# The first half of one 64-channel unit in fp32 from raw weights and a block of ones, with the mean subtracted from the result

## The chip, the cores and the metric

The kernel runs on one core of one Trainium2 chip. A core has a matrix engine (TensorE, "PE" in the profile, its weight loads "PEld"), VectorE (DVE), ScalarE (ACT), GpSimd (POOL), and DMA queues that are issued here from SyncE (SP) and at the start from ScalarE. Each engine works through its own list of instructions in order. The metric is the device time of one execution in microseconds.

## The reference, cut to what matters

```python
def _B_ref(x, w1, w2, w3, w4):                    # x: 2048 tokens x 448 channels
    h = _gelu(_layernorm(x, axis=-1) @ w1)
    c = D // 4
    g0, g1, g2, g3 = the four groups of c = 112 channels of h, shifted by +1, -1, +2, -2 tokens
    hs = jnp.concatenate([g0, g1, g2, g3], axis=-1) @ w2
    x1 = x + hs
    h2 = _gelu(_layernorm(x1, axis=-1) @ w3) @ w4
    return x1 + h2

g = _sigmoid((x * gate_w).sum(-1, keepdims=True))
return g * a + (1 - g) * b                        # a: the state-space part, b: _B_ref
```

The layer norm has no weights. So (x - mean(x)) @ w1 is the same as x @ (w1 - mean of each of its columns), and the factor 1/std of a token can be put on after the product. Written out, the centred product of a token is x @ w1 - sum(x) * mean(column).

## The kernel before, in words

**Tiles and units.** The 2048 tokens are cut into four blocks of 512. For each block there are four units for w1 and, later, 14 units for w3. A w1 unit is one group of output channels. Three of them are filled up to 128 channels with channels of the third group (index 2), so that group 2 is left with 64 channels (`GD = 64`): it is the 64-channel unit. In the order (0, 2, 1, 3) of `units` (L455) the first block's units are number 0 (group 0), 1 (group 2, the 64-channel unit), 2 (group 1) and 3 (group 3); units 4 and 5 belong to the second block.

**Products in two parts.** Each operand is split in a rounded part ("h", type fp32r) and the rest ("l"). A product is a sum over four pieces k of the 448 input channels of w_h x_h, w_l x_h and w_h x_l. Piece 3 has 64 channels only, and its other 64 rows hold its own low part, so a unit has 11 products: h0 to h3, l0 to l3, x0 to x2. In the 64-channel unit the weights' high and low parts stand side by side in the 128 columns of `w1d`, so it has 7 products (h0 to h3, x0 to x2); rows 64 to 127 of its result are copied by ScalarE (`act_add(n, False)`, L485) and added to rows 0 to 63 by VectorE (`act_add(n, True)`).

**The prologue.** Everything up to unit 4 is issued by `begin` (L1119) in an order written out by hand, the table `ORDER` (L1090). Each word is a step of `TASKS` (L1051) or a list of products: `p1:x0a` is unit 1, low part of x, piece 0, first half ("a") of the 512 tokens; "b" is the second half; with no letter, all 512. `s0:21` is unit 0's product with w2 for token tile 2, part 1. Each engine gets its instructions in the order of the words. The steps that the text speaks of:

- `w`: one warm-up matmul on constants (seven more stand ahead of the table).
- `wt` (`presum_unit2`, L917): two additions on VectorE that sum w1 of group 2 over three pieces; `m2` (L927): TensorE turns the sum into column means, the same on every partition, with fp32 matmuls against 1/448; `m0`, `m1`, `m3` (L912, L863): the same for the other groups, `ws` (L907) being a sum for m0. `pe` is the product for the first tokens (L845).
- `c0` to `c3` (`center`, L935): VectorE subtracts the means from w1, in place. `h0` to `h3` and `l0` to `l3`: ScalarE makes the high part, VectorE the low part.
- `xha`, `xhb` (L955) and `xla`, `xlb` (L958): high and low parts of the first block's x, first and second half of its tokens.
- `sa0` to `sa2` (L979) and `sb3` (L971): statistics of x tiles for the layer norm, on ScalarE and VectorE. `ra0`: nine small VectorE steps to 1/std; `ra`, `rm`, `rn` (L360): TensorE turns 1/std into rows.
- `uf0`, `uf1`, `ad1`, `mu0`, `hd0`, `tl0` and so on: copying a unit's result, adding, multiplying by 1/std, the gelu and its two parts. `xh1`, `xl1`: the parts of the second block's x.
- `ld` (L1043): transfers for later blocks.

**Transfers.** `first_loads` (L255) issues the early transfers on the queues of SP and ScalarE. The first block's x comes in three parts of `x0`: pieces 0 and 1 of the first half, pieces 2 and 3 of the first half, and the whole second half. w1 comes group by group, group 2 first.

**Behind the prologue** a loop over units alternates the first products of unit n + 2 with the second products of unit n.

Of the kernel before, what the change touches and what calls it, by code (L numbers as in the profile page):

```python
# [179 lines left out]
def mixer_and_small_steps(ctx, tc, xs, gg, okm, x, xT, xb, x0, w1, w2, w3, w4, gate, par, logdt, dskip, ident, out):  # L180
# [73 lines left out]

    def first_loads():  # L255

        r = raw[0] = room([128, 4 * XW], "raw")
# [11 lines left out]
        sp(w1r[:, 256:512], w1[:, 256:512])
        act(xs[:, 0, :], x[0:128])  # L270
# [6 lines left out]
        sp(r[:, 4 * HW:], x0[:, 4 * HW:])  # L277
# [657 lines left out]
    def center(g, k0=0, k1=4):  # L935
        t = W1R[g][:, k0:k1]
        nc.vector.tensor_tensor(t, t, pm[g][:, None, :].to_broadcast(list(t.shape)), OP.subtract)
# [152 lines left out]
    ORDER = """  # L1090
    w w wt xha w wt m2 w xla m2 ws c2 m0 c2 h2 h2 l2 l2 p1:h0a c0 xha xz p1:x0a sk w xz sa0 xla p1:h2a m1 c0
    h0 xla sa1 l0 p0:x0a p1:x1a p0:h0a c1 p1:x2a h0 p1:h1a,h3a sa0 ld m3 l0 h1 p0:h3a c3 p0:x2a,l2a,l1a sa2
    p0:x1a p2:h1a sb3 p2:x0a p0:h1a,l3a,h2a h3 p2:h2a l1 p2:h3a pe xhb sb3 p3:x2a sb3 p2:x1a xhb p0:l0a
    p2:l2a p0:h0b p3:h2a xlb p2:h0a sa1 p1:h1b p2:x2a p3:h3a p2:h1b sb3 p0:h2b xlb p0:l0b sa2 p2:h0b p1:x0b
    xlb p3:x1b p0:x2b,h1b l3 p0:l1b p2:x0b wh0 p1:x2b p0:x0b p1:h3b ra0 p0:x1b ra0 p0:h3b p2:x2b ra0 p3:h1b
    xh1 p3:l3a ra0 p3:x2b p2:l0a ra0 p2:l0b ra0 xh1 p1:h0b p3:h2b ra0 p3:l2b p2:x1b ra0 p0:l3b xh1 ra0
    p2:h3b p1:x1b sk p1:h2b wl0 p0:l2b xh1 p3:l1a ra sk uf0 sk p2:l2b xl1 rm p2:l1a p3:x0b uf1 p3:l0b mu0
    p3:x0a sk p4:l1 mu0 p4:h1 sk ad1 p2:h2b hd0 p3:l3b,h0b p4:h3 hd0 mu0 p3:l2a mu1 p2:l1b bm p2:l3a mu1
    p3:h3b hd0 p3:x1a,h1a,l1b hd0 p4:l2 xl1 s0:00 hd0 s0:10 p5:h3 xl1 hd0 p4:x0 s0:01 ba p5:h0 sb7 s0:20 hd0
    hd1 p2:l3b tl0 s0:21 p3:l0a p5:x1 sb7 wh2 mu2 s0:30 p5:x0 cp1 p4:h2 sb5 p3:h0a s0:02 wh1 p4:h0 tl0 s0:11  # L1100
    sb5 s0:31 tl1 hd2 s0:22 p5:h2 p4:l3 wl2 hd2 p5:h1 hd2 s0:12 sb7 p4:x1 cp2 s1:11,31 sb5 s1:20 cp2 s1:01
    sb7 s0:32 sb5 s2:30 tl2 s1:30,10 s2:20 ra1 mu3 s2:00 s1:21 s2:22 ra1 s1:00 wl1 hd3 p4:l0 s2:10 ra1 wh3
    s2:02 ra1 s2:01 ra1 s2:31 hd3 xl1 hd3 s2:11,32,21 ra1 cp3 s2:12 ra1 p4:x2 ra1 wl3 p5:x2 s3:30 uf5 s3:20
    ra1 tl3 s3:00 rn sb9 s3:01 bn s3:12,31 ad5 s3:02 cp3 s3:21,10 mu4 s3:22,32,11 re hd4 re hd4 hd4 mu5 cp4
    re cp4 hd5 tl4 cp5 sb9 re
# [196 lines left out]
```

## Time and profile before

| | us |
|---|---|
| median of 3 runs (370.73 to 371.57) | 371.1 |
| the profiled execution | 370.7 |
| its span, first to last instruction | 368.9 |
| TensorE busy | 363.4 (99%) |
| VectorE busy | 308.1 (84%) |
| ScalarE busy | 215.9 (59%) |
| GpSimd busy | 63.3 (17%) |

The profile is of one execution, with times from the first instruction on. In a timeline a row is: start, duration, engine, line, operation, what it writes and reads, shapes, how many instructions are merged, and in brackets how long the engine idled before it and what ended that. Matmuls are pipelined: a duration is that of one matmul from start to end, and several overlap, so the pace is read from start to start. "[0.63 <-DMA raw<-x_in]" means that ScalarE idled 0.63 us until a transfer into the tile `raw` had landed. In the table of stretches each row is a stretch, its length, and the busy time of PE, PEld, DVE, ACT and POOL with the number of instructions, the granted clock of TensorE, the busy share of the DMA engines and GB/s.

### The profile page before, as it was taken

What the parts mean: (1) busy time and instruction counts of PE and PEld (TensorE: products, weight loads), DVE (VectorE), ACT (ScalarE), POOL (GpSimd) and SP (SyncE); (2) the same over time, 40 slices, a digit from 0 to 9 for tenths busy, and PEclk for the clock granted to TensorE, in tenths of its full rate; (3) what the DMA queues carried; (4) which work ended last, traced back from release to release, by engine and by line L of the source; (5) the groups of instructions that cost most, each with busy time, mean ns of one, the idle gap of its engine ahead of it and who ended that gap; (6) DMA issues with size and microseconds to landing.
All of it is one profiled execution on the core that took longest, in us unless ns stands there. A gap on an engine that the chain in (4) does not pass through costs nothing.

```text
span 368.9 us, 5308 instructions
## 1 busy us (share of the span) xinstructions
PE 363.4 (99%) x1734; PEld 314.3 (85%) x1734; DVE 308.1 (84%) x571; ACT 215.9 (59%) x383; POOL 63.3 (17%) x176
## 2 busy tenths in 40 slices
PE   8999999999999999999999999999999999999995
PEld 4988888888888888888888888888888888888885
DVE  4999979797999997378799899998789999998533
ACT  5987668777684637944274774554756645455220
POOL 1000432000300000110013433224243234000000
PEclk9999999999999999999999999999999999999999
DMA  7994116626948064001833514457385611361213
GB/s 258 393 398 157 38 65 124 134 88 251 390 134 203 0 116 156 0 0 52 178 107 77 89 28 94 114 165 131 83 131 121 179 16 28 79 179 30 64 50 105
DMA packets 88479, 46.14 MB, mean 125 GB/s; under 512 B 67200, under 2 KB 82944, under 8 KB 87808
## 3 DMA queue, kind: packets, MB, share of 16 engines
q1 hardware_dynamic: 88016, 45.27, 45.6%
q10 hardware_dynamic: 432, 0.49, 0.4%
q8 instruction: 15, 0.25, 0.3%
q14 instruction: 16, 0.13, 0.1%
HBM read 34.74 MB, written 11.01 MB: 124 GB/s over the span
## 4 chain that ended last, share of the span: by engine, by line
PE 93%; DMA 4%; ACT 1%; DVE 0%; ACTq 0%; SPq 0%; issue 0%
PE p L478 46%; PE acc L603 45%; DMA raw<-xb_in 2%; DMA xs<-x_in 2%; PE acc L638 1%; ACT xh L394 1%; PE p L638 0%; PE misc L363 0%; DVE xh L401 0%; ACT uf L996 0%; ACTq L268 0%; DVE uf L1007 0%; SPq L279 0%; ACT ug L1020 0%; ACT ug L1023 0%
## 5 line engine op out<-in xcount | busy, mean ns | idle before, releaser
L539 ACT ACTIVATE uf<-p 128x512 f32<-128x512 f32 x56 | 33.4, 597 | 113.3 <-PE p L478 113.2
L478 PE MATMUL p<-xh,w3l 128*128 128x512 f32 x224 | 70.1, 394 | 0.0
L478 PE MATMUL p<-xh,w3h 128*128 128x512 f32 x224 | 70.1, 394 | 0.0
L758 DVE TENSOR_TENSOR_SCAN z<-z,carry 128x512 f32<-128x512 f32 x48 | 61.5, 1282 | 4.2 <-POOL z L752 0.5
L603 PE MATMUL acc<-w4l,uh 128*128 128x448 f32 x216 | 56.3, 367 | 0.0
L603 PE MATMUL acc<-w4h,uh 128*128 128x448 f32 x216 | 56.0, 365 | 0.0
L603 PE MATMUL acc<-w4h,ul 128*128 128x448 f32 x216 | 55.8, 364 | 0.0
L569 DVE TENSOR_TENSOR ul<-uf,uh 128x512 fp32r<-128x512 f32 x56 | 38.1, 681 | 20.1 <-ACT uh L549 20.0
L478 PEld LDWEIGHTS p<-xh,w3l 128*128 128x128 f32 x224 | 42.1, 188 | 9.8
L478 PE MATMUL p<-xl,w3h 128*128 128x512 f32 x168 | 47.7, 392 | 0.0
L478 PEld LDWEIGHTS p<-xh,w3h 128*128 128x128 f32 x224 | 42.1, 188 | 6.6
L603 PEld LDWEIGHTS acc<-w4h,uh 128*128 128x128 f32 x216 | 40.5, 188 | 6.0
L603 PEld LDWEIGHTS acc<-w4h,ul 128*128 128x128 f32 x216 | 40.6, 188 | 3.5
L603 PEld LDWEIGHTS acc<-w4l,uh 128*128 128x128 f32 x216 | 40.6, 188 | 3.4
L753 ACT ACTIVATE z<-zs,nu 128x512 f32<-128x512 f32 x64 | 42.3, 710 | 0.6 <-DMA zs<-xT_in 0.6
L478 PEld LDWEIGHTS p<-xl,w3h 128*128 128x128 f32 x168 | 31.5, 188 | 7.2
L549 ACT ACTIVATE uh<-uf 128x512 fp32r<-128x512 f32 x56 | 35.4, 633 | 1.8
L752 POOL COPY z<-carry 128x1 f32<-128x1 f32 x48 | 32.1, 679 | 16.0 <-DVE zs L764 15.9
L760 POOL COPY carry<-z 128x1 f32<-128x1 f32 x48 | 13.1, 273 | 105.7 <-DVE z L758 105.0
L344 POOL TENSOR_TENSOR t<-r 128x4 f32<-128x4 f32 (+1 forms) x5 | 3.1, 627 | 117.4 <-DVE r L343 117.4
L603 PE MATMUL acc<-w2l,uh 128*128 128x448 f32 x64 | 19.9, 368 | 0.0
L758 DVE TENSOR_TENSOR_SCAN z<-z,carry,zero 128x512 f32<-128x512 f32 x16 | 19.9, 1247 | 0.0
(207 smaller groups left out, 541.8 us busy)
## 6 DMA issues: line engine op xcount, KB each, us to landing
zs<-xT_in SPq DMA_DIRECT2D x4, 1024.0 KB, 8.3
yd<-yt SPq DMA_DIRECT2D x56, 64.0 KB, 2.0
ysb<-yd SPq DMA_DIRECT2D x16, 224.0 KB, 2.7
raw<-xb_in SPq DMA_DIRECT2D x3, 1032.0 KB, 12.6
raw<-w_in SPq DMA_DIRECT2D x3, 1024.0 KB, 5.6
xd<-xt SPq DMA_DIRECT2D x16, 192.0 KB, 2.1
xr<-xd SPq DMA_DIRECT2D x16, 192.0 KB, 3.1
raw<-w_in SPq DMA_DIRECT2D x3, 896.0 KB, 4.6
```

Source lines behind the costliest of these rows:

```text
L344: eng.tensor_mul(t, y, y)
L394: nc.scalar.activation(XH["a", b][:, k, :], raw[b][:, k, :], AF.Copy)
L478: nc.tensor.matmul(p[:, t0:t1], (wl if w else wh)[:, k, :], (xl if x_ else xh)[:, k, o + t0:o + t1], start=(q == 0 and fresh), stop=stop i ...
L539: nc.scalar.activation(UF[n], P1[n], AF.Gelu_apprx_tanh)
L549: nc.scalar.activation(UH[n], UF[n], AF.Copy)
L569: nc.vector.tensor_sub(UL[n], uf, f32(UH[n]))
L603: nc.tensor.matmul(ACC[j], (UL if p == 2 else UH)[n][:, t], wl if p == 1 else wh, start=first_, stop=last_)
L638: nc.tensor.matmul(acc, (UL if p == 2 else UH)[m][:, t], (wl if p == 1 else wh)[:, c], start=q == last and m == n and p == 0, stop=m > n a ...
L752: nc.gpsimd.tensor_copy(z4[:, m, 0:1], carry[:, k, m:m + 1])
L753: nc.scalar.activation(z4[:, m, 1:], ZS[b][:, k, :], AF.Copy, scale=nu[:, k, m:m + 1])
L758: nc.vector.tensor_tensor_scan(z, z, up, carry[:, k, m:m + 1], OP.add, OP.add)
L760: nc.gpsimd.tensor_copy(carry[:, k, m:m + 1], z[:, TB - 1:])
```

## The change

For the first half of the first block's tokens, the 64-channel unit is no longer computed from centred and split weights. GpSimd writes ones into a 128 x 4 x 64 block and VectorE copies the raw w1 of that unit beside it (`w1f`, which lies in the memory of the last two x tiles until these are loaded). Four fp32 products on raw x (`p1:f0a` to `p1:f3a`) give sum(x) in rows 0 to 63 and x @ w1 in rows 64 to 127. ScalarE writes the negative means of 64 columns, VectorE turns them into a column on 64 partitions with two 32 x 32 transposes (`nm`), and the final addition becomes two instructions: for the first half result + sum * (-mean), for the second half the addition as before. The seven half products of unit 1's first half go; centring and splitting stay, since the second half needs them.

On SP's queue the second part of x0 is issued ahead of the second half of group 0's w1 instead of behind it. The transfer of the last x tiles becomes a second step of `ld`, further on. Two warm-up matmuls go, and the table of steps is a new one.

```diff
+    w1f = xs[:, L // 128 - 2:, :].rearrange("p a b -> p (a b)")[:, :512].rearrange("p (k m) -> p k m", k=4)
+    mt = big.tile([GD, GD + 32], F32, name="mt")
+    mrow, mcol = mt[:, :GD], mt[:, GD:]
...
         act(w1r[:, :256], w1[:, :256])
+        sp(r[:, 2 * HW:4 * HW], x0[:, 2 * HW:4 * HW])
         sp(w1r[:, 256:512], w1[:, 256:512])
         act(xs[:, 0, :], x[0:128])
-        sp(r[:, 2 * HW:4 * HW], x0[:, 2 * HW:4 * HW])
...
     def constants():
+        nc.gpsimd.memset(w1f[:, :, :GD], 1.0)
...
+    def mean_turned():
+        nc.scalar.activation(mrow, pm[2][:GD, :], AF.Copy, scale=-1.0)
+        yield
+        for o in (0, 32):
+            nc.vector.transpose(mcol[o:o + 32, :], mrow[o:o + 32, o:o + 32])
+            yield
+
+    def first_add():
+        uf, p, h = UF[1], P1[1], TB // 2
+        nc.vector.scalar_tensor_tensor(uf[:GD, :h], p[:GD, :h], mcol[:, 0:1], uf[:GD, :h], op0=OP.mult, op1=OP.add)
+        nc.vector.tensor_add(uf[:GD, h:], p[:GD, h:], uf[:GD, h:])
...
         load_xt(2)
-        load_x(3 * NT + 1, L // 128)
         gate_load()
...
-        w=each(*((warm_up, 1) for _ in range(5))),
+        w=each(*((warm_up, 1) for _ in range(3))),
-        ad1=each((act_add, 1, True)),
+        nm=mean_turned(), cw=each((nc.vector.tensor_copy, w1f[:, :, GD:], W1R[2])), ad1=each((first_add,)),
-        ld=each((more_loads,)),
+        ld=each((more_loads,), (load_x, 3 * NT + 1, L // 128)),
...
     ORDER = """
+    w w wt xha m2 wt cw m2 w nm p1:f1a c2 xla h2 xha nm ws xla sa0 xla m0 l2 p1:f2a sa0 c0 sk xz xz c2
+    p1:f3a c0 h0 m1 nm h0 l0 h2 l0 sa1 ld p0:l0a c1 m3 sa2 l2 p1:f0a c3 h1 p0:h0a sb3 p2:x2a h3 p0:h1a
+    p2:h1a p0:h3a sb3 p0:l2a xhb sb3 p3:x0a pe sa2 xlb p0:l1a,x0a,l1b p1:h0b p0:l3a sb3 xhb p2:h3a l1 p0:x2a
+    p1:x1b p3:h0a p0:l0b sa1 p0:h0b xlb p0:x0b p3:h2a p0:l2b xlb p3:h0b p2:x1a wh0 p0:x1b ra0 p1:h1b p2:x0a
+    ra0 p3:h1a p2:l0b ra0 p0:l3b ra0 p0:h2b l3 xh1 p2:h2a ld p0:x1a p2:l2b,h0b p0:h3b xh1 p1:h2b ra0 p3:x1b
+    ra0 p3:l0a p2:l1a ra0 xh1 p0:x2b wl0 p1:h3b p0:h2a,h1b p1:x2b xh1 ra0 p1:x0b p3:h3a ra0 p3:x1a p2:h1b sk
+    uf0 rm xl1 ra uf1 p2:l3b mu0 p3:l2b sk p3:l2a mu0 p3:x2a wh3 p2:h2b p3:l0b sk sk p4:h0 ad1 sk hd0 p4:h3
+    mu0 p2:x1b mu1 wh2 p4:h1 p2:l0a,l2a hd0 p3:h2b xl1 p3:l3a,l1a p4:h2 hd0 p2:x0b sb5 bm p5:h0 hd0
+    p2:h0a,l3a p5:h3 tl0 hd0 p2:h3b,x2b mu1 p5:h2 hd0 p5:x0 p4:l3 tl0 hd1 s0:10 p3:h1b xl1 p5:h1 ba s0:20
...
     def products(n, codes):
...
-            left = LEFT.setdefault(n, (14 if n == 1 else 22) if n < 4 else 11 if n == 4 else 7) - 1
+            left = LEFT.setdefault(n, (11 if n == 1 else 22) if n < 4 else 11 if n == 4 else 7) - 1
+            if c[0] == "f":
+                k = int(c[1])
+                if n not in P1:
+                    P1[n] = ps.tile([128, TB], F32, name="p1", tag="p1", bufs=3)
+                r = slice(0, 64 if k == 3 else 128)
+                nc.tensor.matmul(P1[n][:, :TB // 2], w1f[r, k, :], parts0[0][r, k, :TB // 2], start=left == 10,
+                                 stop=not left)
+                continue
```

The old table, for the counts of the prediction, from its start to the first products with w2:

```
w w wt xha w wt m2 w xla m2 ws c2 m0 c2 h2 h2 l2 l2 p1:h0a c0 xha xz p1:x0a sk w xz sa0 xla p1:h2a m1 c0
h0 xla sa1 l0 p0:x0a p1:x1a p0:h0a c1 p1:x2a h0 p1:h1a,h3a sa0 ld m3 l0 h1 p0:h3a c3 p0:x2a,l2a,l1a sa2
p0:x1a p2:h1a sb3 p2:x0a p0:h1a,l3a,h2a h3 p2:h2a l1 p2:h3a pe xhb sb3 p3:x2a sb3 p2:x1a xhb p0:l0a
p2:l2a p0:h0b p3:h2a xlb p2:h0a sa1 p1:h1b p2:x2a p3:h3a p2:h1b sb3 p0:h2b xlb p0:l0b sa2 p2:h0b p1:x0b
xlb p3:x1b p0:x2b,h1b l3 p0:l1b p2:x0b wh0 p1:x2b p0:x0b p1:h3b ra0 p0:x1b ra0 p0:h3b p2:x2b ra0 p3:h1b
xh1 p3:l3a ra0 p3:x2b p2:l0a ra0 p2:l0b ra0 xh1 p1:h0b p3:h2b ra0 p3:l2b p2:x1b ra0 p0:l3b xh1 ra0
p2:h3b p1:x1b sk p1:h2b wl0 p0:l2b xh1 p3:l1a ra sk uf0 sk p2:l2b xl1 rm p2:l1a p3:x0b uf1 p3:l0b mu0
p3:x0a sk p4:l1 mu0 p4:h1 sk ad1 p2:h2b hd0 p3:l3b,h0b p4:h3 hd0 mu0 p3:l2a mu1 p2:l1b bm p2:l3a mu1
p3:h3b hd0 p3:x1a,h1a,l1b hd0 p4:l2 xl1 s0:00 hd0 s0:10 p5:h3 xl1 hd0 p4:x0 s0:01 ba p5:h0 sb7 s0:20 hd0
...
```

More of the change, by code (lines that the diff above doesn't have):

```diff
@@ L1051, in mixer_and_small_steps @@
     TASKS = dict(
-        ws=each((presum,)), m0=each((presum_mean,)), w=each(*((warm_up, 1) for _ in range(5))),
+        ws=each((presum,)), m0=each((presum_mean,)), w=each(*((warm_up, 1) for _ in range(3))),
         xha=each((x_hi, 0, lh), (x_hi, 2, lh)), xhb=each((x_hi, 0, rh), (x_hi, 2, rh)),
@@ L1065, in mixer_and_small_steps @@
         ra0=rstd_ops(r1, 0, NT + 1), ra1=rstd_ops(r1, NT + 1, 2 * NT + 1),
-        uf0=each((first_copy,)), uf1=each((act_add, 1, False)), ad1=each((act_add, 1, True)),
+        uf0=each((first_copy,)), uf1=each((act_add, 1, False)), nm=mean_turned(), cw=each((nc.vector.tensor_copy, w1f[:, :, GD:], W1R[2])), ad1=each((first_add,)),
         mu0=first_mul_ops(0), mu1=first_mul_ops(1), hd0=first_head_ops(), tl0=first_tail_ops(),
@@ L1069, in mixer_and_small_steps @@
         uf5=each((act_add, 5, False)), ad5=each((act_add, 5, True)),
-        ld=each((more_loads,)), re=each(*((residual, 3, j) for j in range(NT))),
+        ld=each((more_loads,), (load_x, 3 * NT + 1, L // 128)), re=each(*((residual, 3, j) for j in range(NT))),
     )
@@ L1090, in mixer_and_small_steps @@
     ORDER = """
[L1091 to L1105, printed above, removed]
+    w w wt xha m2 wt cw m2 w nm p1:f1a c2 xla h2 xha nm ws xla sa0 xla m0 l2 p1:f2a sa0 c0 sk xz xz c2
@@ new lines, in mixer_and_small_steps @@
+    uf0 rm xl1 ra uf1 p2:l3b mu0 p3:l2b sk p3:l2a mu0 p3:x2a wh3 p2:h2b p3:l0b sk sk p4:h0 ad1 sk hd0 p4:h3
+    mu0 p2:x1b mu1 wh2 p4:h1 p2:l0a,l2a hd0 p3:h2b xl1 p3:l3a,l1a p4:h2 hd0 p2:x0b sb5 bm p5:h0 hd0
+    p2:h0a,l3a p5:h3 tl0 hd0 p2:h3b,x2b mu1 p5:h2 hd0 p5:x0 p4:l3 tl0 hd1 s0:10 p3:h1b xl1 p5:h1 ba s0:20
+    p4:x0 xl1 hd0 p2:l1b cp1 p3:x0b p4:l2,l1 mu2 wh1 s0:30 p3:l3b s0:32 sb7 s0:00 hd2 s0:31 p4:x1 sb5 sb5
+    p4:l0 hd2 hd2 s0:01 p3:x2b sb7 p5:x2 sb7 s0:21 cp2 p5:x1 wl2 p3:h3b s0:22 cp2 p3:l1b sb7 s2:00 sb5 tl1
@@ L1106, in mixer_and_small_steps @@
+    s0:02 s2:30 s0:11 ra1 p4:x2 tl2 s0:12 s1:11 s2:20 ra1 mu3 s1:30 s2:02,10 ra1 s2:32 wl1 hd3 s2:22
+    s1:00,21 ra1 uf5 s1:10 ra1 s1:01 ra1 hd3 s2:21 ra1 hd3 wl3 s1:20 s2:12,11 ra1 cp3 s1:31 ra1 ad5 s2:31,01
+    cp3 rn tl3 s3:30 bn s3:20 sb9 s3:00,01,10 mu4 s3:32,11,02 sb9 mu5 hd4 s3:31,12,22 re s3:21 hd4 hd4 re
+    cp4 re hd5 tl4 cp4 cp5 re
     """
```

## The prediction

> **What bounds the kernel now.** I read the engine totals, the chain that ended last, the busy time by stretches, and then what TensorE waits for.
>
> ```profile
> PE 363.4 (99%) x1734; PEld 314.3 (85%) x1734; DVE 308.1 (84%) x571; ACT 215.9 (59%) x383; POOL 63.3 (17%) x176
> ...
> PE 93%; DMA 4%; ACT 1%; DVE 0%; ACTq 0%; SPq 0%; issue 0%
> ```
>
> ```profile
> 4.50:10.50 6.00, 5.17 (x36) 4.37 (x37) 5.02 (x15) 4.20 (x13) 0.45 (x3) 1.00 1.04 360
> 10.50:20.00 9.50, 9.50 (x83) 9.16 (x83) 8.64 (x27) 8.13 (x19) 0.80 (x3) 1.00 1.01 389
> ...
> 36.00:350.00 314.00, 314.00 (x1455) 272.29 (x1454) 271.70 (x481) 187.14 (x318) 61.07 (x154) 1.00 0.43 107
> ```
>
> TensorE runs without a gap from 36 to 350 us (314.00 of 314.00), at a clock of 1.00. Nothing behind the prologue can hide or win anything, so a prologue that ends x us later moves the end by x. The change edits the prologue alone. The question is when TensorE has finished the first units' products.
>
> The prologue isn't evenly bound. From 10.5 us TensorE is full; before, it has holes that warm-up matmuls partly cover. Later there is one place where it waits, for the first products with w2:
>
> ```profile
> 13.07 0.55 PE L478 MATMUL p<-xh,w1h 128*128 128x256 f32 x3
> ...
> 17.50 0.60 PE L363 MATMUL misc<-idt,r 128*128 128x128 f32 x4
> ...
> 20.43 0.52 PE L478 MATMUL p<-xh,w1l 128*128 128x256 f32 x2
> 21.02 0.67 PE L603 MATMUL acc<-w2h,uh 128*128 128x448 f32 x2
> 21.53 0.39 PE L478 MATMUL p<-xh,w1d 128*128 128x512 f32 x1
> ```
>
> In the table of steps the first product on the second half of the tokens ("b") is p0:h0b, in the row at 13.07. From there to the transposes at 17.50 stand 37 half products: 4.43 / 37 = **0.12 us each**. The row at 20.43 holds p3:l1b (a half, 0.12) and p4:l2 (whole, 0.23 by the pitch from 21.53 on). They are streamed by 20.78, and s0:00 starts at 21.02: 0.24 us are lost there.
>
> **The gate.** The b half of block 0 is one transfer, the third part of x0, and ScalarE splits it:
>
> ```profile
> raw<-x_in SPq DMA_DIRECT2D x1, 512.0 KB, 6.4
> ```
> ```profile
> 5.89 0.47 SPq L277 DMA_DIRECT2D raw<-x_in  x1
> ```
> ```profile
> 11.58 0.63 ACT L940 ACTIVATE w1h<-w1r 128x512 fp32r<-128x512 f32 x1 [0.25 <-DVE w1r L937]
> 12.32 1.15 ACT L956 ACTIVATE xh<-raw 128x512 fp32r<-128x512 f32 x2
> ```
> ```profile
> L956 ACT ACTIVATE xh<-raw x4: 617/634/636, 4.2 to 12.9; 128x520 fp32r<-128x520 f32 x2, 128x512 fp32r<-128x512 f32 x2
> ```
>
> It lands at 5.89 + 6.4 = 12.29, the split starts at 12.32 and takes 0.62, so it is done at 12.95, and with about 0.05 from one engine to the next no b product can start before **13.0**. Before, p0:h0b started at 13.07, right behind other work: gate and work met.
>
> **The change part by part.** *Work moved behind the gate.* Units 0 to 3 have 22 + 14 + 22 + 22 = 80 half products before. In the old table 25 stand ahead of p0:h0b (unit 0: 11, unit 1: 7, unit 2: 6, unit 3: 1), so 55 are left at the gate. In the new table unit 1 has 7 half products and four fp32 products, 73 + 4 in all. The first b product is now p0:l1b, and ahead of it stand the four fp32 products and only 10 halves (unit 0: 7, unit 2: 2, unit 3: 1): 63 are left. The means and the first-token product stand ahead of the gate in both; transposes, units 4 and 5 and the w2 products behind it. So 8 x 0.12 = **0.96 us more work behind the gate**. It opens at 13.0 instead of 13.07: **-0.07**.
>
> *What the fp32 products cost themselves.* No 256-column fp32 product is in this trace. The nearest rows are the column means, fp32 of 128 columns:
>
> ```profile
> 8.07 1.05 PE L867 MATMUL pm<-w1r,cm 128*128 128x128 f32 x8
> 8.88 0.37 PE L478 MATMUL p<-xl,w1h 128*128 128x256 f32 x1
> ```
>
> Four products are recorded as eight instructions and take 8.88 - 8.07 = 0.81, or 0.20 each; with twice the columns about 0.41 (bounds 0.20, if columns cost nothing, and 0.48, four halves). Four take 1.6 to 1.9 and replace 7 x 0.12 = 0.84. This lies ahead of the gate, where TensorE has holes, so it costs nothing if the early chain still reaches p0:l1b by 13.0. That has to be walked.
>
> *The early chain.* SP now issues the second part of x0 (k = 2, 3) ahead of 128 KB of w1 (unit 0, k = 2, 3).
>
> ```profile
> raw<-x_in SPq DMA_DIRECT2D x2, 260.0 KB, 4.5
> ...
> xs<-x_in ACTq DMA_DIRECT2D x1, 224.0 KB, 5.6
> ...
> w1r<-w_in SPq DMA_DIRECT2D x1, 128.0 KB, 3.6
> ```
> ```profile
> 1.66 0.45 ACTq L270 DMA_DIRECT2D xs<-x_in  x1
> ```
> ```profile
> 1.19 0.42 SPq L269 DMA_DIRECT2D w1r<-w_in  x1
> ```
> ```profile
> 7.16 0.64 ACT L956 ACTIVATE xh<-raw 128x520 fp32r<-128x520 f32 x1 [0.63 <-DMA raw<-x_in]
> 7.70 0.56 ACT L981 ACTIVATE xn<-xs 128x448 f32<-128x448 f32 x1
> ...
> 8.26 0.40 ACT L940 ACTIVATE w1h<-w1r 128x256 fp32r<-128x256 f32 x1
> 8.56 0.56 ACT L981 ACTIVATE xn<-xs 128x448 f32<-128x448 f32 x1
> ...
> 9.43 0.65 ACT L983 ACTIVATE xn<-xs,st 128x448 f32<-128x448 f32 x1
> ...
> 10.13 0.63 ACT L940 ACTIVATE w1h<-w1r 128x512 fp32r<-128x512 f32 x1
> ```
>
> ```profile
> 4.71 0.23 DVE L924 TENSOR_TENSOR ws<-ws,w1r 128x64 f32<-128x64 f32 x1
> ...
> 15.77 0.17 DVE L321 TENSOR_TENSOR t<-r 128x5 f32<-128x5 f32 x1
> 15.97 0.17 DVE L323 SCALAR_TENSOR_TENSOR t<-t,v 128x5 f32<-128x5 f32 x1
> ```
>
> Part two landed at 7.1 (ScalarE's row at 7.16 waits for it). With 128 KB less ahead at 360 GB/s (window above) it gains some 0.4; I take 6.6 (bounds 5.5 and 7.1). The w1 piece, landed at 1.19 + 3.6 = 4.8 before, now follows it, near 6.9. The copy of w1 starts when VectorE is done with the sums (4.71 + 0.23) and, with 256 columns like the 0.41 rows below, ends at 5.3. TensorE does f1a by 5.8, waits about 1 us for that w1 piece, then does m0, f2a, f3a and m1 until 9.3. The next product, p0:l0a, needs w1l of unit 0: split of part two on ScalarE until 7.3; on VectorE two low parts, l2, half of c0 (done 8.9), half of c2, c0's other half, a transpose, then l0. With the durations of these rows:
>
> ```profile
> L943 DVE TENSOR_TENSOR w1l<-w1r,w1h 128x512 fp32r<-128x512 f32 x2 | 1.4, 683 | 0.0
> ...
> L943 DVE TENSOR_TENSOR w1l<-w1r,w1h 128x256 fp32r<-128x256 f32 x2 | 0.8, 423 | 0.0
> L937 DVE TENSOR_TENSOR w1r<-w1r,pm 128x256 f32<-128x256 f32 x2 | 0.8, 414 | 0.0
> ...
> L943 DVE TENSOR_TENSOR w1d<-w1r,w1d 128x128 fp32r<-128x128 f32 x2 | 0.5, 289 | 0.2 <-ACT w1d L940 0.2
> ...
> L961 DVE TENSOR_TENSOR xh<-raw,xh 64x256 fp32r<-64x256 f32 x1 | 0.4, 422 | 0.0
> ```
>
> that is 10.0. m3 and f0a follow until 11.4. ScalarE has the statistics of tile 0 (landing 1.66 + 5.6 = 7.3; 0.56 and 0.70 apart in the rows), then h0 twice, h2, two more statistics and h1: 0.3 + 0.3 + 0.25 + 0.56 + 0.56 + 0.6 from about 9, so h1 is done near 11.8, h3 near 12.5, the split of the b half near 13.1. p2:x2a needs h1, p3:x0a needs h3; then come the first-token product (0.3) and two halves. p0:l1b comes at 12.8 (part two at 6.0) to 13.35 (at 6.6). Behind the gate's 13.0 I charge **+0.2** (bounds 0 and 0.5).
>
> *VectorE behind the gate.* The transposes of r ("ra") need nine small steps, 0.2 apart in the rows; ahead of them VectorE has, from 13.0 or a little later, also the low parts of b (1.5), l1 and l3 (1.2 to 1.4) and one low part of w2 (0.5): some 5.1 us, so 18.1 to 18.3. TensorE arrives at 18.0 to 18.2: **+0.15** (0 to 0.4). The added copy of w1, the two 32x32 transposes and the split addition (two of 256 columns for one of 512) lie in VectorE's time before 13 or beside full TensorE work; if that cover goes, they are 0.3, 0.4 and 0.15.
>
> *The lost 0.24.* Behind the gate the new table has 56 halves, 9 whole products and five transposes ahead of s0:10, 6.7 + 2.1 + 0.5 = 9.3 us. TensorE arrives at 22.5 or later, when the input (ready at 21.0) is there: **-0.24**.
>
> *At nothing.*
>
> ```profile
> POOL xz L966 <- DMA raw<-x_in: 5.6, 1, 5.6
> ```
>
> GpSimd's memset of the ones lies in these 5.6 us of waiting; without that cover it would hold f1a back by a few tenths, and f1a has 1 us to spare. Two warm-up matmuls go, both fillers ahead of 8 us. The transfer of the last x tiles now waits for f0a behind three short transfers on SP's queue; only the last block needs it, and it is issued well before SP turns to block 3.
>
> Sum: 0.96 - 0.07 + 0.2 + 0.15 - 0.24 = **+1.0 us**. The profiled execution took 370.7 (span 368.9 and 1.8 around it), so 371.7; against the median of 371.1, which is 0.4 higher, **372.1**.
>
> **The rivals.** *The early chain is late.* If part two lands as before (7.1), or h1 and h3 slip, every 0.1 behind 13.35 is 0.1 at the end; 0.5 to 1.5 more gives 372.6 to 373.6. Against it: the transfer has less ahead of it than before.
>
> *The gate opens earlier.*
>
> ```profile
> GB/s 0 0 0 0 0 0 0 141 158 153 203 194 348 359 378 373 363 268 252 236 277 243 348 347 322 432 391 412 388 390 358 423 394 323 334 383 376 395 398 434
> ```
>
> Each number is a quarter of a us. From 4.25 to 5.5 the queues moved about 255 GB/s, later 390. If the new order of transfers fills that dip, 1.25 x (1 - 255/390) = 0.4 us are won, the b half lands at 11.9, and with the waits gone the sum is 0.96 - 0.4 - 0.24 plus 0 to 0.3: +0.3 to +0.6, 371.4 to 371.7, within 0.2%.
>
> *The prologue gets faster.* One mechanism: the fp32 products fill the holes before 10.5 and the whole table moves up. Dense from f1a at 5.4, TensorE would be at p0:l1b at 11.0. Then s0 would be the bound (input at 21.0), and behind it the new table has less work (7 halves and 9 whole products against 3 and 14: 0.7 us): 370.4. It decides at a first b product before 12.2, a landing before 11.5; 10.8 for more than 0.2%. Against it: bytes ahead of that transfer are the same, and the dip is worth 0.4.
>
> *The clock drops.* TensorE now waits about 1 us near 6 and again near 9.5. The trace shows 1.00 throughout 4.5 to 10.5, with 0.8 us of holes in that stretch (6.00 less 5.17). The start shows what a slow array is like:
>
> ```profile
> 2.86 0.15 PEld L903 LDWEIGHTS <-const-bfloat16-1.0 128*128 128x128 bf16 x1 [0.28 <-issue]
> 3.29 0.61 PEld L903 LDWEIGHTS <-const-bfloat16-1.0 128*128 128x128 bf16 x3 [0.28 <-issue]
> ```
>
> The warm-up matmuls of 512 columns come 0.43 apart until 3.29, from 0.77 on; whole products later take 0.23. Another 2.5 us at about half pace would add up to 1.3: 373.4. The Trainium skill, "TensorE: Matmul & The Clock Gate", Part 1, says that an idle window of about 3.4 us throttles the clock and as long a busy one frees it; by that rule waits of 1 us would not do it, which speaks for the small chance.
>
> **How the numbers follow.** Forecast (+0.5 to +1.5) 0.52; early chain late 0.15; gate earlier 0.18; faster 0.12; clock 0.03. About 0.2% (0.74 us) is what a measurement of this kernel can tell from no change. Slower by more: 0.41 of the forecast's 0.52, and the late chain and the clock, 0.59; within: 0.11 + 0.18 = 0.29; faster 0.12. The range leaves out the faster rival's lower half and what lies beyond 1.9 us: 370.9 to 373.0.
>
> **What would show it.** Right: the first b half product at 13.0 to 13.4, TensorE idle near 6 and 9.5, no wait at the first w2 product, the prologue's end 1 us later. Wrong: the b half landing before 11.9, p0:l0a before 9.3, or a TensorE that runs dense from f1a. A changed pace behind 36 us would show an effect that I don't see.

## The result, and the profile after

The changed kernel took **372.62 us** (median of 19 runs, 371.93 to 376.38) beside 371.57 for the kernel before (median of 19, 370.73 to 372.42): a ratio of **1.0042, 95% interval 1.0028 to 1.0057**. A second comparison (a1 below) gave 372.44 beside 371.32, ratio 1.0025 (1.0015 to 1.0036). So the change costs 0.9 to 1.6 us by the two ratios (0.0025 and 0.0042 of 371.3 and 371.6) and 1.1 by both pairs of medians. Four of the 19 executions of the changed kernel took 373.8 to 376.4, at mean granted clocks of 0.988 to 0.997; the second comparison has none above 373.2. The forecast was +1.0 us. Its direction was right; its size lies just below what the first comparison allows (+1.04 to +2.1) and inside what the second does (+0.6 to +1.3). Its 372.1 stood on a median of 371.1 from three runs; beside the 371.57 of this comparison it is only 0.5 more.

The engine totals and the chain that ended last, on the page of the changed kernel:

```profile
PE 365.5 (98%) x1733; PEld 315.5 (85%) x1733; DVE 308.8 (83%) x575; ACT 216.6 (58%) x384; POOL 64.4 (17%) x177
...
PE 95%; DMA 3%; ACT 0%; ACTq 0%; SPq 0%; DVE 0%; issue 0%
```

The same stretches of busy time as before, with the one behind 350 us added; then that stretch for the kernel before:

```profile
4.50:10.50 6.00, 5.88 (x31) 4.49 (x31) 5.02 (x17) 4.43 (x14) 0.45 (x3) 1.00 1.04 375
10.50:20.00 9.50, 8.53 (x71) 7.73 (x69) 7.56 (x24) 7.33 (x17) 0.07 (x1) 1.00 1.02 383
...
36.00:350.00 314.00, 314.00 (x1455) 272.20 (x1454) 272.37 (x481) 187.67 (x321) 62.25 (x154) 1.00 0.43 106
350.00:372.00 22.00, 17.36 (x88) 15.45 (x86) 8.10 (x13) 3.54 (x6) 0.00 (x0) 0.99 0.24 81
```

```profile
350.00:372.00 22.00, 15.21 (x77) 13.44 (x75) 7.07 (x12) 2.46 (x4) 0.00 (x0) 0.95 0.20 65
```

From 36 to 350 us nothing differs (314.00 of 314.00, 1455 matmuls in both). What the prologue lost stands unchanged at the end: 17.36 less 15.21 = 2.15 us more TensorE work is left behind 350. The new holes lie between 10.5 and 20 us, where TensorE was full before and now stands still for 0.97 us.

Where they are is in TensorE's timeline of the changed kernel:

```profile
9.94 0.39 PE L482 MATMUL p<-xh,w1l 128*128 128x256 f32 x1
...
12.66 0.38 PE L482 MATMUL p<-xl,w1h 128*128 128x256 f32 x1 [0.26 <-ACT w1h L957]
12.97 0.40 PE L849 MATMUL pe<-w1r,xz 128*2 128x32 f32 x8
...
13.52 0.29 PE L482 MATMUL p<-xl,w1h 128*128 128x256 f32 x1
14.51 0.38 PE L482 MATMUL p<-xh,w1l 128*128 128x256 f32 x1 [0.70 <-ACT xh L973]
...
19.50 0.71 PE L367 MATMUL misc<-idt,r 128*128 128x128 f32 x5
...
24.15 0.37 PE L607 MATMUL acc<-w2h,uh 128*128 128x448 f32 x1
```

The rows at 13.52 and 14.51 are p0:x0a and the first b product, p0:l1b. By the pace of 0.12 TensorE could have had it at 13.64; it waited for ScalarE's split of the b half, which had waited for the third part of x0. The chain that ended last, over the first 24 us, says why that part was late:

```profile
1.17 5.00 DMA w1r<-w_in
...
6.19 0.39 SPq L246
...
6.62 7.19 DMA raw<-x_in
...
13.83 0.64 ACT xh L973
...
14.51 5.15 PE p L482 x39
```

A piece of w1 that ScalarE's queue issued at 1.17 landed at 6.17. Only then does SP issue x tiles 3 and 4 (L246), and behind them the third part of x0, at 6.62 instead of 5.89. It lands at 13.81 instead of 12.29. SP's waits in the first 9 us, changed kernel and then kernel before (us in total, times, the longest):

```profile
SPq L246 <- DMA w1r<-w_in: 2.3, 2, 1.4
```

```profile
SPq L246 <- DMA w1r<-w_in: 1.4, 1, 1.4
SPq L278 <- DMA xs<-x_in: 0.9, 1, 0.9
```

Before, SP's issues of x tiles are held by such a landing once; now twice. The trace also gives the reason. It records for each transfer the semaphore that tells of its landing: the early transfers of both queues use eight semaphores in turn, in the order of the program, and every issue from the ninth to the 19th waits for the semaphore that it is about to use again, which is that of the transfer eight places ahead. This holds in all 17 profiles of this case. The w1 piece on ScalarE's queue is the third transfer, x tiles 3 and 4 are the eleventh, the third part of x0 is the twelfth. (The line of L278 is the thirteenth, held by the fifth, x tile 0.) In the five profiles with the old order of transfers the third one lands at 4.72 to 5.02 and the eleventh is issued at 4.91 to 5.36, not held; in the twelve with the new order, where 260 KB instead of 128 KB are issued next to it, it lands at 6.04 to 6.81 and the eleventh is issued right behind, at 6.05 to 6.83.

### The profile page after: what moved, and what is told of

The parts are those of the page before. It is cut to its first block, busy times and chain, and to the rows that moved or that the text cites. A ratio compares the mean times of both kernels' runs of the same rounds, so it can differ in the third digit from the quotient of the medians.

```text
span 371.1 us, 5317 instructions
## 1 busy us (share of the span) xinstructions
PE 365.5 (98%) x1733; PEld 315.5 (85%) x1733; DVE 308.8 (83%) x575; ACT 216.6 (58%) x384; POOL 64.4 (17%) x177
## 4 chain that ended last, share of the span: by engine, by line
PE 95%; DMA 3%; ACT 0%; ACTq 0%; SPq 0%; DVE 0%; issue 0%
PE p L482 48%; PE acc L607 45%; DMA raw<-x_in 2%; DMA w1r<-w_in 1%; PE acc L642 1%; PE misc L367 0%; PE p L642 0%; ACT xh L973 0%; ACTq L267 0%; SPq L246 0%; DVE xs L631 0%; PE misc L739 0%
## 5 line engine op out<-in xcount | busy, mean ns | idle before, releaser
L756 POOL COPY z<-carry 128x1 f32<-128x1 f32 x48 | 33.6, 711 | 16.0 <-DVE zs L768 15.9
L764 POOL COPY carry<-z 128x1 f32<-128x1 f32 x48 | 12.8, 266 | 104.3 <-DVE z L762 103.5
L607 PE MATMUL acc<-w2h,uh 128*128 128x448 f32 x64 | 20.1, 367 | 0.0
## 6 DMA issues: line engine op xcount, KB each, us to landing
raw<-xb_in SPq DMA_DIRECT2D x3, 1032.0 KB, 12.5
```

The costliest lines, as they stand in the source:

```text
L607: nc.tensor.matmul(ACC[j], (UL if p == 2 else UH)[n][:, t], wl if p == 1 else wh, start=first_, stop=last_)
L756: nc.gpsimd.tensor_copy(z4[:, m, 0:1], carry[:, k, m:m + 1])
L764: nc.gpsimd.tensor_copy(carry[:, k, m:m + 1], z[:, TB - 1:])
```

## The experiments

Fifteen runs follow, each beside the kernel before. One column of the table needs a word. As TensorE is full from the prologue's end on, the time at which its **last matmul** starts shows how late the prologue ended, free of what the output transfers add behind it. It is 364.94 in the profile of before. The rule of the prediction would give it from two numbers, the start of the first b product and the halves left at that point: 0.12 us for each half above 55, plus the start's distance from 13.07, less 0.24 where the wait ahead of the first w2 product is gone.

| kernel | ratio to before (95%) | first b product / halves left | last matmul, later by | by the rule |
|---|---|---|---|---|
| changed | 1.0042 (1.0028 to 1.0057) | 14.51 / 63 | 2.14 | 2.16 |
| a1, changed again | 1.0025 (1.0015 to 1.0036) | 13.62 / 63 | 1.25 | 1.27 |
| b1, before again | 1.0011 (0.9999 to 1.0022) | 13.26 / 55 | 0.21 | 0.19 |
| e1 | 1.0045 (1.0032 to 1.0058) | 14.54 / 63 | 1.87 | 2.19 |
| e2 | 1.0023 (1.0012 to 1.0033) | 14.60 / 55 | 1.41 | 1.29 |
| e3 | 1.0047 (1.0034 to 1.006) | 14.39 / 55 | 1.48 | 1.08 |
| e4 | 1.0055 (1.004 to 1.0069) | 14.04 / 63 | 1.90 | 1.69 |
| e5 | 1.0025 (1.0013 to 1.0036) | 14.73 / 55 | 1.31 | 1.42 |
| e6 | 1.0006 (0.9993 to 1.0019) | 13.51 / 55 | 0.54 | 0.44 |
| e7 | 1.0047 (1.0028 to 1.0066) | 15.21 / 63 | 2.83 | 2.86 |
| e8 | 1.0038 (1.0025 to 1.0051) | 13.48 / 63 | 1.02 | 1.13 |
| e9 | 1.0056 (1.0035 to 1.0077) | 13.93 / 63 | 1.88 | 1.58 |
| e10 | 1.0037 (1.0024 to 1.005) | 13.47 / 63 | 1.03 | 1.12 |
| e12 | 1.0023 (1.0012 to 1.0033) | 13.76 / 55 | 0.80 | 0.69 |
| e13 | 1.0066 (1.0045 to 1.0087) | 15.06 / 63 | 2.39 | 2.71 |

The rule holds to 0.12 in ten of the 15 profiles and to 0.4 in all. (e11, whose filled wait it doesn't cover, is told below: ratio 1.0009, first b product at 13.44, last matmul 0.47 later.) What differs from kernel to kernel is when the gate opens and how much is left behind it.

**b1, the kernel before against itself**, tells how far such numbers carry. It was run late, for the question whether the forecast had read a usual execution.

> The kernel before, itself: ratio 1.000, 0.9990 to 1.0010. If the profile from which the forecast was made shows a usual execution: third part of x0 landed at 12.1 to 12.5, first b half product of block 0 at 13.0 to 13.2, span 368.9 to 369.2. If it was one of its fastest: third part landed at 12.6 to 13.2, first b half product at 13.4 to 14.0, span 369.4 to 370.

TensorE's timeline of it; the row at 13.26 begins with the first b product:

```profile
13.26 0.53 PE L478 MATMUL p<-xh,w1h 128*128 128x256 f32 x3
...
21.20 0.68 PE L603 MATMUL acc<-w2h,uh 128*128 128x448 f32 x2
```

Between the two expectations: third part split from 12.29 on, first b product at 13.26, first w2 product 0.18 later than in the first profile, but a span of 369.8, 0.9 longer. The rest is behind TensorE (last section). The identical kernel gave 1.0011 (0.9999 to 1.0022): differences of 0.1% to 0.2% between two of these kernels are not told apart here.

**a1, the changed kernel again.**

> The changed kernel itself again, as the common measure of the three runs beside it on the same chip: ratio to the kernel before 1.003 to 1.0055. Its profile tells how far the landing of the third part of x0 (13.8 us in the first profile) moves from execution to execution.

Its chain over the first 24 us:

```profile
1.17 4.91 DMA w1r<-w_in
...
6.09 0.39 SPq L246
...
6.52 6.39 DMA raw<-x_in
...
13.62 5.14 PE p L482 x39
```

The same chain with the same hold of SP, but the transfer took 6.39 us where it had taken 7.19. The loss is 1.25 instead of 2.14.

**e6: the fp32 products alone**, in the old table and with the old order of transfers. The beginning of the table, against the kernel before:

```diff
-    w w wt xha w wt m2 w xla m2 ws c2 m0 c2 h2 h2 l2 l2 p1:h0a c0 xha xz p1:x0a sk w xz sa0 xla p1:h2a m1 c0
+    w w wt xha wt m2 cw xla m2 w nm ws c2 p1:f0a m0 c2 h2 h2 l2 l2 p1:f1a c0 xha xz sk xz sa0 xla nm p1:f2a
...
```

> The fp32 products alone: the table and the order of transfers of the kernel before, with f0 to f3, the copy of w1, the two transposes and the split addition in place of unit 1's seven half products (two warm-up matmuls fewer, the last x tiles' transfer right behind the others). If the fp32 products lie in TensorE's early holes, as the prediction says, the time is that of the kernel before: ratio 0.9990 to 1.0010. Rival: the fp32 products cost what they add (0.9 us): 1.0015 to 1.003.

1.0006 (0.9993 to 1.0019): no difference that can be told from none; the interval allows up to 0.7 us. Its timeline of TensorE shows the products at full price:

```profile
7.36 1.03 PE L1135 MATMUL p<-raw,xs 128*128 128x256 f32 x4
8.23 1.05 PE L871 MATMUL pm<-w1r,cm 128*128 128x128 f32 x8
```

Two products, recorded as four instructions, take 8.23 less 7.36 = 0.87, or 0.43 each. They lie ahead of the gate. In this profile the first b product comes at 13.51 all the same, 0.25 behind b1's, and the last matmul is 0.33 later than b1's: a cost of some 0.3 us is not excluded. The greater part of the loss belongs to the table or the order of transfers.

**e2 and e12: the order of the two transfers alone**, in the kernel before and in e6.

```diff
+        sp(r[:, 2 * HW:4 * HW], x0[:, 2 * HW:4 * HW])
         sp(w1r[:, 256:512], w1[:, 256:512])
         act(xs[:, 0, :], x[0:128])
-        sp(r[:, 2 * HW:4 * HW], x0[:, 2 * HW:4 * HW])
```

> The kernel before with nothing but the two transfers on SP's queue swapped as in the change. Gate theory: SP's later transfers are held back, the third part of x0 lands at 12.8 to 13.8, the first b half product moves from 13.07 to 13.5 to 14.5, and 0.4 to 1.4 us of that reach the end (ratio 1.001 to 1.004). Rival 'chance': ratio 1.000. Rival 'early chain': the second part of x0 lands 0.7 us sooner and the kernel gets faster, 0.998 to 0.999.

> The old table with the fp32 products, and the change's order of the two transfers of SP: the corner of table and order that no run has yet. If the order of transfers holds the prologue (SP's issue of x tiles 3 and 4 waits for the w1 piece, so that the third part of x0 is issued about 0.8 us late): third part issued at 6.6 to 6.8, first b half product of block 0 at 13.9 to 14.6, ratio 1.0015 to 1.003 to the kernel before. If the second part's earlier issue is worth something to the fp32 products, or the order matters only with the old computation: first b product near 13.5 and ratio 0.9995 to 1.001.

TensorE's timeline of e2:

```profile
7.01 0.71 PE L915 MATMUL pm<-w1r,cm 128*128 128x128 f32 x4 [1.57 <-DMA w1r<-w_in]
...
14.60 0.62 PE L478 MATMUL p<-xh,w1h 128*128 128x256 f32 x3 [1.05 <-ACT xh L956]
```

With nothing but the swap, `m0` waits 1.57 us for its w1, SP is held as in the changed kernel (third part issued at 6.76, landed at 13.89), and TensorE idles 1.05 at the gate: 1.0023, with the last matmul 1.41 later. Here the order that the forecast had called equal turns out to cost 0.1% to 0.2% (b1 had 1.0011 for no change at all, so the time alone would not show it; the trace does). e12 gave 1.0023 too, against 1.0006 without the swap, which is the time that was expected from the held issue. But its first b product came at 13.76, earlier than expected, without a wait for the split. In that profile it was the early chain that was late, not the gate: `m0` at 6.86 and `m3` at 10.44, 0.16 and 0.26 later than in e6. As 0.15 of that is there already at `m2` (4.78 after 4.63), it isn't shown that the swap made this chain late.

**e1: the changed kernel with the old order**, the same two lines moved back.

> The changed kernel with SP's old order of transfers (second part of x0 behind the second half of group 0's w1), all else as changed. Gate theory: the third part of x0 is issued near 5.9 us and lands near 12.3 again, the first b half product (p0:l1b) starts at 13.0 to 13.5 instead of 14.5, and the kernel stays 0.7 to 1.2 us slower than before (ratio 1.002 to 1.003). Rival 'chance': the late landing in the changed kernel's profile has nothing to do with the order of issue, the ratio stays near 1.004. Rival 'early chain': what counts is when the second part of x0 lands, now near 7.1 instead of 6.4, so it gets slower still, 1.005 or more.

Its timeline of TensorE:

```profile
10.84 0.39 PE L482 MATMUL p<-xh,w1l 128*128 128x256 f32 x1 [1.03 <-DVE w1l L960]
...
13.56 0.38 PE L482 MATMUL p<-xl,w1h 128*128 128x256 f32 x1 [0.27 <-ACT w1h L957]
13.87 0.40 PE L849 MATMUL pe<-w1r,xz 128*2 128x32 f32 x8
```

No gain: 1.0045. The third part is now issued at 5.48 and landed at 12.21, but the second part of x0 lands at 7.35, VectorE comes to unit 0's low part of w1 later, p0:l0a waits 1.03 for it, and the first-token product is reached at 13.87 instead of 12.97. The new table needs the second part early; getting it early makes `m0` and the third part late. The four corners, with the fp32 products:

| | old order | new order |
|---|---|---|
| old table | 1.0006 (e6) | 1.0023 (e12) |
| new table | 1.0045 (e1) | 1.0042, 1.0025 (the change) |

The table costs 0.4% with the old order; the order costs 0.1% to 0.2% with the old table; together they cost no more than the table alone.

**e7 and e9: the new table and order without the fp32 products** (seven half products of the old computation in their place), e9 with four more warm-up matmuls ahead of `m0`.

```diff
...
-    p1:f3a c0 h0 m1 nm h0 l0 h2 l0 sa1 ld p0:l0a c1 m3 sa2 l2 p1:f0a c3 h1 p0:h0a sb3 p2:x2a h3 p0:h1a
+    p0:l0a c1 m3 sa2 l2 p1:h0a,x0a,h1a,x1a,h2a,x2a,h3a c3 h1 p0:h0a sb3 p2:x2a h3 p0:h1a p2:h1a p0:h3a sb3
...
```

> The new table and order of transfers with the old computation: the seven half products of unit 1's first half stand where f0a stood, no fp32 products, no copy, no transposes. If the cost is the table's and the transfers', not the fp32 products', the ratio is that of the changed kernel within 0.3 us, 1.003 to 1.0045. Rival: the fp32 products are the cost and it comes back to 1.000 to 1.0015.

> As e7 (new table, old computation), with four warm-up matmuls in TensorE's wait ahead of m0. In e7's profile the means run at 0.21 us an instruction, half the pace of the other runs (0.10 to 0.11), from 7.3 to about 12.6. If that is the array's slow pace, caused by the 1.2 us without work, the warm-ups keep it at 0.11 and the kernel is 0.8 to 1.5 us faster than e7: ratio 1.001 to 1.0025. Rival: the slow pace has nothing to do with the wait; the warm-ups delay m0 by up to 0.3 us and the ratio stays at 1.004 to 1.005.

1.0047 and 1.0056: the loss is there without any fp32 product. Whether the table is worse without them isn't told by intervals that overlap with 1.0042. TensorE's timeline of e7, and behind it that of e9, showed a second thing:

```profile
4.56 0.64 PE L934 MATMUL pm<-w1r,cm 128*128 128x64 f32 x2
...
7.27 1.22 PE L918 MATMUL pm<-w1r,cm 128*128 128x128 f32 x4 [1.19 <-DMA w1r<-w_in]
8.28 0.63 PE L918 MATMUL pm<-ws,cm 128*128 128x128 f32 x2
8.71 1.92 PE L870 MATMUL pm<-w1r,cm 128*128 128x128 f32 x8
```

```profile
4.47 0.41 PE L934 MATMUL pm<-w1r,cm 128*128 128x64 f32 x2 [0.31 <-DMA w1r<-w_in]
...
6.72 0.71 PE L918 MATMUL pm<-w1r,cm 128*128 128x128 f32 x4 [0.30 <-DMA w1r<-w_in]
7.27 0.39 PE L918 MATMUL pm<-ws,cm 128*128 128x128 f32 x2
```

In e7 four of these instructions take 1.01 (7.27 to 8.28), 0.25 each, where e9 shows 0.14; e7's matmuls run at about half pace until 13 us. In e9 they are at full pace, and the time was no better: there the third part of x0 opened the gate at 13.93. But the two differ already at `m2` (0.64 and 0.41), ahead of the wait that e9's warm-up matmuls fill, so this pair doesn't show what the filling did.

**e3, e5, e11: work put where TensorE waits.** e3 moves eight a products ahead of the first b product, e5 also two low parts of w1 on VectorE; e11 moves four products of e6 ahead of the first w2 product.

```diff
...
-    p2:h1a p0:h3a sb3 p0:l2a xhb sb3 p3:x0a pe sa2 xlb p0:l1a,x0a,l1b p1:h0b p0:l3a sb3 xhb p2:h3a l1 p0:x2a
+    p2:h1a p0:h3a sb3 p0:l2a xhb sb3 p3:x0a pe sa2 xlb p0:l1a,x0a p0:x2a p2:h3a p3:h0a p3:h2a p2:x1a p2:x0a
+    p3:h1a p2:h2a p0:l1b p1:h0b p0:l3a sb3 xhb l1 p1:x1b p0:l0b sa1 p0:h0b xlb p0:x0b p0:l2b xlb p3:h0b wh0
...
```

> The changed kernel with eight half products of the first token half moved from behind p0:l1b to just ahead of it; nothing else. Gate theory: they fill TensorE's wait for the third part of x0 (0.87 us in the profile), 55 half products are left behind the gate as in the kernel before, and the end comes 0.7 to 0.9 us sooner than in the changed kernel (ratio to the kernel before 1.001 to 1.002). Rival 'early chain': TensorE has no idle time there that counts, since later steps wait for VectorE and ScalarE, and the ratio stays near 1.004.

> As e3 (eight half products moved ahead of p0:l1b), and VectorE's l1 and l3 moved ahead of its first low part of the b half. Theory of two gates: the third part holds TensorE and VectorE alike; VectorE idles before it and then needs 3.6 us to l3, on which p3:l0a waits (e3's profile). With that work done in VectorE's idle time the 0.7 us of e3 now reach the end: ratio 0.6 to 0.9 us below the changed kernel, 1.002 to 1.003. Rival: the bound lies elsewhere, or the early chain holds everything, and it stays within 0.2 us of the changed kernel.

> As e6 (old table and transfers with the fp32 products), with four products that don't need the first gelu moved ahead of s0:00 and p0:l2b moved forward by two words. If TensorE's wait at the first w2 product (0.24 us before, some 0.3 in e6) is a loss of its own, it goes: 0.2 to 0.4 us below e6, ratio 0.9990 to 1.0002. Rival: the wait only moves to the next products that need the gelu, ratio as e6, 1.0005.

None gained what was expected. In e3 55 halves are left at the gate, as before the change, but TensorE arrives at `pe` at 12.76 (12.17 in the kernel before), and further on it waits for VectorE, as its chain shows:

```profile
16.77 0.61 DVE w1l L960
...
17.42 1.57 PE p L482 x11
```

In e5 that wait is gone, but w1's piece landed later in the profiled execution (`m0` waits 1.22) and `pe` comes at 13.11. Its first b product came 0.22 later than in the changed kernel's first profile and its last matmul 0.83 earlier; by the rule eight halves moved ahead are worth 0.74 there. e11 closed the hole of 0.24 ahead of the first w2 product and ended no earlier than e6: its last matmul is 0.07 earlier, as much as its first b product.

**e4, e8, e10, e13: one part of the chain made earlier.** e4 issues the third part ahead of x tiles 3 and 4; e8 puts `m3` and p1:f0a ahead of p0:l0a; e10 adds three warm-up matmuls ahead of `m0`; e13 issues the w1 piece on ScalarE's queue.

```diff
-        load_x(3, 5)
         sp(r[:, 4 * HW:], x0[:, 4 * HW:])
+        load_x(3, 5)
...
-    p1:f3a c0 h0 m1 nm h0 l0 h2 l0 sa1 ld p0:l0a c1 m3 sa2 l2 p1:f0a c3 h1 p0:h0a sb3 p2:x2a h3 p0:h1a
+    p1:f3a c0 h0 m1 nm h0 l0 h2 l0 sa1 ld m3 p1:f0a p0:l0a c1 sa2 l2 c3 h1 p0:h0a sb3 p2:x2a h3 p0:h1a
...
-        sp(w1r[:, 256:512], w1[:, 256:512])
+        act(w1r[:, 256:512], w1[:, 256:512])
```

> The changed kernel with the third part of x0 issued ahead of x tiles 3 and 4 instead of behind them. Gate theory: it lands some 1.2 us sooner (448 KB less ahead of it), near 12.5, the first b half product starts at 13.2 to 13.7, and the end comes 0.5 to 1.0 us sooner than in the changed kernel (ratio 1.0015 to 1.003). Rival 'early chain': the statistics of tiles 3 and 4, now landing later, hold VectorE up ahead of the low parts of b, nothing is won, 1.004.

> The changed kernel with m3 and f0a moved ahead of p0:l0a, on which TensorE waits for VectorE's l0 while m3's weights are there. Theory of the early chain (the table sets how early h1 and h3 are made, whatever the transfers do): c3 and h3 come 0.2 to 0.4 us sooner, and where the third part has landed by then the end comes as much sooner: ratio 0.0005 to 0.001 below the changed kernel's 1.0025 to 1.004. Rival: the third part alone sets the end, no gain.

> The changed kernel with three warm-up matmuls in TensorE's wait ahead of m0, nothing else. If some of its executions lose time to a slow array in the first 12 us (four of the first 19 took 373.8 to 376.4 us, none of the kernel before over 372.5), the long ones go and the ratio falls to 1.0015 to 1.0025. Rival: the pace is not part of the cost; the same spread, ratio 1.0025 to 1.004.

> The changed kernel, with the second half of group 0's w1 issued right behind its first half on ScalarE's queue, ahead of x tile 0. If SP's held issue and the wait of the first mean for w1 make the prologue late: the first mean has no wait or a shorter one, the early chain ends 0.5 to 1 us earlier, and the time falls by 0.3 to 0.7 us (ratio 1.0015 to 1.0025). If the statistics of tile 0 or the third part of x0 decide instead: no gain, ratio 1.003 to 1.005, with first b half product still at 13.5 to 14.5.

e4's chain shows the wait handed on: x tiles 3 and 4 now land at 12.97, VectorE's statistics of them hold up the low part of b, and p1:x1b waits for it.

```profile
7.15 5.83 DMA xs<-x_in
...
15.00 4.42 PE p L482 x34
```

e8 and e10 have their first b product at 13.48 and 13.47 without a wait there, as have e5 and e13; TensorE is then bound by the early chain, with `pe` at 12.82 and 12.81. TensorE's timeline of e10:

```profile
12.49 0.38 PE L482 MATMUL p<-xl,w1h 128*128 128x256 f32 x1 [0.27 <-ACT w1h L957]
12.81 0.40 PE L849 MATMUL pe<-w1r,xz 128*2 128x32 f32 x8
...
13.47 0.31 PE L482 MATMUL p<-xh,w1l 128*128 128x256 f32 x1
```

Neither time can be told from that of the changed kernel. Whether e10's warm-up matmuls prevent long executions, which was its question, stays open: its longest took 373.34, and a1's, without them, 373.14. e13 went the wrong way: on ScalarE's queue the w1 piece landed later, and x tile 0 behind it too. TensorE's and ScalarE's timelines of e13:

```profile
7.79 0.71 PE L919 MATMUL pm<-w1r,cm 128*128 128x128 f32 x4 [1.29 <-DMA w1r<-w_in]
```

```profile
9.09 0.58 ACT L998 ACTIVATE xn<-xs 128x448 f32<-128x448 f32 x1 [1.82 <-DMA xs<-x_in]
```

Moving this piece to the other queue thus didn't make it early, in the one profile taken. The Trainium skill, "DMA: Bandwidth & Descriptors", section "Issuing engines are not separate DMA queues", says that transfers from any issuing engine run on the same 16 DMA engines, so that a second issuer saves issue time only; this run agrees in that it shows no gain (first use of the piece at 7.79; 6.58 to 7.51 in the profiles with the new order that leave it on SP's queue). No version beat the kernel before; e6 and e11 equal it within their intervals.

## Why the prediction was right and where it was wrong

- **Nothing behind the prologue hides or wins anything: right.** 314.00 of 314.00 in both; the last matmul moves by what the prologue loses.
- **0.96 us more work behind the gate: right.** From the first b product to the first w2 product stand 9.64 us in the changed kernel (14.51 to 24.15), 9.3 forecast, and the rule with this term fits all kernels that have 63 halves left to 0.32. e5, which moves eight halves back ahead of the gate, gets them back.
- **The fp32 products cost nothing: right as far as it can be told**, by e6, whose interval allows 0.7 us and whose profile shows some 0.3; 0.43 each where 0.41 was put.
- **The gate opens at 13.0, worth -0.07: this step failed.** The first b product came at 14.51 in the first profile and at 13.62 in the second: +1.44 and +0.55 instead of -0.07. The prediction counted the bytes ahead of the third part of x0, found them the same and kept its landing at 12.29. It didn't walk SP's queue with its waits: with the second part of x0 ahead, the w1 piece on ScalarE's queue lands at 6.17, SP's issue of x tiles 3 and 4, eight transfers on, waits for that landing, and the third part is issued 0.6 to 0.7 us late and landed 0.6 to 1.5 late. e2 shows this wait, made by the swap alone, and the third part lands at 12.02 to 12.32 in the five profiles with the old order, at 12.53 to 13.89 in the eleven with the new (e4, which moves it, left out). The hold isn't all of it: in e5, e7 and e13 it was issued latest, at 7.16 to 7.25, and landed first among the eleven, at 12.53 to 12.60. What else the new order does to this landing stays open.
- **The early chain reaches p0:l1b between 12.8 and 13.35, charged +0.2: too early.** It would have had it at 13.64, and at 13.35 in a1. The prediction tied 12.8 to a second part of x0 landed at 6.0; it landed at 5.97 and at 5.87 in a1, so the chain is 0.84 and 0.55 longer than put. p0:l0a came at 9.94 where 10.0 was forecast, and h3 was done at 12.60 where 12.5 was; p3:x0a, `pe` and two halves behind it then took 1.04 where 0.12, 0.3 and 0.24 were put. In both profiles the late gate covers this. Where the gate isn't late (e8, e10) this chain binds by itself and costs 0.4, within the bound of 0.5. So there are two ways to lose behind 13.0, and mending one shows the other.
- **0.15 for VectorE ahead of `ra`: not there.** The transposes start at 19.50 without a wait.
- **The lost 0.24 disappears: it did** in the changed kernel, whose first w2 product has no wait in front of it. e11 shows that this alone needn't be worth 0.24.
- **TensorE idle near 6 and 9.5**, a sign of being right: in a1 it idles 0.55 near 6. In the first profile it was busy for 5.88 of the 6.00 us from 4.5 to 10.5, which looks like the sign of being wrong (dense from f1a), but the table didn't move up for it: f1a itself took 0.70 (5.88 to 6.58), at half pace, and `m0` started at 6.58 in both. Near 9.5 the eight instructions from 8.66 on need 0.81 by the rate of before, and the next product started 1.28 behind their start, so some 0.5 were idle there.
- **The rivals of an earlier gate and a faster prologue** didn't happen: the b half landed at 13.81 and 12.91, where they needed less than 11.9.
- **The clock's rival**, another 2.5 us at half pace, happened in part. In the first profile `m2`'s two rows take 0.64 and 0.67 where they took 0.41 and 0.40 before, and ScalarE gets the means at 5.70 instead of a1's 5.42; the early chain is 0.29 later than a1's, which the late gate hid. e7, which isn't the changed kernel, shows it in full.

In the profiled execution the sum is thus 0.96 + 1.44 (14.51 less 13.07) - 0.24 = 2.16, in a1 0.96 + 0.55 - 0.24 = 1.27, where the forecast had 1.0. The 0.2 and the 0.15, put down for other waits, happen to make up for a part of the gate's 0.55 and 1.44; that the total came near is to that extent luck. One more term hides in the start: the profile that the forecast was added to was an early one. Measured from b1, whose last matmul is 0.21 later, the two losses are 1.93 and 1.04. Why the medians show only 1.1 would take more profiles than were taken; a landing as late as 13.81 was seen in two of the eleven.

## What to carry to other kernels

When a transfer changes its place in a queue, walk every later issue of that queue with its waits, not only the bytes. Find out which semaphore each issue waits for: here it was that of the transfer eight places ahead, on whichever queue, and a later landing there held the issue on which the gate hangs. Where a prologue has two chains of nearly equal length, a change to one is worth only the distance to the other; measure a table and an order of transfers apart and together before adding them up. And a forecast of a few tenths of a per cent needs the kernel before profiled more than once.

## What the runs showed of the hardware

**The same transfer lands at different times.** Issued at 6.62 and 6.52 in two executions of the same kernel, the third part of x0 took 7.19 and 6.39 us; TensorE's last matmul differs by 0.89.

**The end behind TensorE varies as much.** The last matmuls of before and of b1, from their timelines:

```profile
364.94 0.28 PE L638 MATMUL p<-w4h,ul 128*128 128x128 f32 x1
```

```profile
365.15 0.28 PE L638 MATMUL p<-w4h,ul 128*128 128x128 f32 x1
```

They are 0.21 apart, the spans (368.9 and 369.8) 0.9: from the last matmul's start to the end are about 4.0 and 4.6 us, and 5.4 in e5. What stands there are VectorE's last additions and the output's transfers. Single executions of one kernel differ by 1.8 us (370.64 to 372.47 in b1); how much of that lies in this stretch, two profiles don't tell, but of the 0.9 between them it has the greater part.

**TensorE at half pace with a granted clock of 1.00.** In e7 the matmuls ran at about half pace until 13 us, through a wait of 1.19; yet the granted clock of that run is 0.999 in the mean. The Trainium skill, "TensorE: Matmul & The Clock Gate", Part 1, has the array start at half rate and come up after one busy window of about 3.4 us, whose start is not tied to the kernel's. By that figure a busy window would be over at the latest 6.8 us after the wait's end at 7.27, at 14.1 (an estimate from that page); the 13 us agree. The wait didn't bring the slow stretch on: `m2` ahead of it was slow already, as it was in the changed kernel's first profile, where full pace came at about 6.6 without such a wait. Whether the wait prolonged it was not shown.
